# The fourth batch's softmax blocks turned by VectorE and moved by ScalarE, spread over two passes

## The chip, the cores and the metric

The kernel runs on one core of a Trainium2 chip. The metric is device time in microseconds (us) for one execution. The engines of the core are TensorE (PE, matrix products; its weight loads are listed apart as PEld), VectorE (DVE), ScalarE (ACT), GpSimd (POOL) and SyncE (SP, which here only issues transfers). Each works through its own queue in order, and they meet through semaphores.

## The reference

An attention with 32 learned memory slots per head, and on its output a mixture of 8 experts. Eight batches of 576 tokens, 8 heads of 64 features, so the model width is 512; experts have 1024 hidden units.

```python
def _attn_ref(q, k, v, phi):                      # phi: batch, head, token, 32 slots
    a = np.exp(phi - np.max(phi, axis=2, keepdims=True))     # softmax over the tokens
    a = a / (np.sum(a, axis=2, keepdims=True) + 1e-09)
    k_m = np.einsum('bhsm,bhsd->bhmd', a, k)      # 32 keys and values per head
    v_m = np.einsum('bhsm,bhsd->bhmd', a, v)
    scores = scale * np.matmul(q, k_m.transpose(0, 1, 3, 2))
    ...                                           # softmax over the 32 slots: attn
    return np.matmul(attn, v_m)

def _moe_ref(x, expert_emb, tau, w1, w2):
    ...                                           # cosine router: expert and gate of each token
    h = np.maximum(x[mask] @ w1[e], 0.0)
    out[mask] = gate_w[mask, None] * (h @ w2[e])
```

What matters here is the first softmax, over the tokens: its exponentials `exp(phi - max)` of one batch are 8 x 32 rows of 576 tokens, and the products with k and v contract over the tokens, so the exponentials are needed with the tokens on the partitions.

## The kernel before

The batches go through a software pipeline. Pass b (`batch(b, ...)`) runs the two layers of the chosen expert for batch b on TensorE and, between their steps, everything that later batches need. The first layer (`first`) has 16 steps of six matmuls (tiles ph, line 751); the second (`second`) has 40 steps: one half tile of 64 tokens x 2 and four full tiles of 128 tokens (py), eight steps each. In pass 0 the half tile comes first, in passes 1 to 6 behind the first full tile. `steps(b, t, u)` is an order written out by hand: a list of work for each place of `first` and `second`, which is emitted behind the matmuls of that step. An engine's queue therefore holds its instructions in exactly this order.

A tile py is emptied by ScalarE (ys, line 796), which multiplies by the gate. Four PSUM banks (`mm`) are used in rotation by ph, py and the four tiles pg of `project` (line 732), with which the next pass begins. `project` multiplies the first-layer weights by the slots' values; ScalarE casts each pg to gh (line 734), VectorE takes the rest gl (line 735), and both feed the first layer. Ahead of pg, at the start of pass 1, stand the transposes tk and tv; behind it the products ts and tl of the next batch's attention.

For batch m the exponentials are made in place in the buffer ex: `load_phi` brings phi, `largest` takes the maximum of a half (nm, line 481, VectorE), `softmax` the exponential with its sums (line 496, ScalarE). They are brought into the layout eT (tokens on partitions) in one of two ways:

- by TensorE (`blocks` and `flip`): 18 transposes into PSUM (line 533, tiles po and te) and four ScalarE copies (line 536);
- by VectorE and ScalarE (`blocks_of` and `by_token`): VectorE transposes 32 x 32 blocks of each half into xt (line 542), then ScalarE makes 16 moves, each a pair of copies that changes partitions (lines 550 and 552). The generator `self.moves` hands them out one at a time.

`slots` (line 574, from `gather`) then sums over the tokens. Before the change the first way serves the third batch (in pass 0) and the fourth batch (in pass 1, second-layer place 7); the second way serves the batches from the fifth on. The fourth batch's phi is issued by SyncE, at second-layer place 27 of pass 0; its maxima are taken at first-layer places 2 and 4 of pass 1 and its exponentials at second-layer places 0 and 1.

Other names that the steps touch: `norm` (line 181, VectorE, ea with sums s) and `root` and `gates` (ss, n, l; lines 248 to 279) compute the gates of the next batch's tokens. The power in `root` is GpSimd's, and l is an exponential on ScalarE. `parts` splits the attention weights (aT: a cast on VectorE, line 711, and a subtraction on GpSimd, line 712). At the end of pass 0 GpSimd sends out ys and then splits the next pass's second-layer weights (wh, wl).

Of the kernel before, what the change touches and what calls it, by code (L numbers as in the profile page):

```python
# [20 lines left out]
B, H, S, D, M = 8, 8, 576, 64, 32  # L21
N, DM, E, FF = B * S, H * D, 8, 1024
NG = 2
# [264 lines left out]
class Kernel:  # L288
# [136 lines left out]
    def load_phi(self, b, gs=range(NG)):  # L425
        if b < B:
            for g in gs:
                to = self.e(b, g)
                if g and 1 < b < 4:
                    self.nc.sync.dma_start(to[:, 64:], self.phiT[b, :, g, : 4 * P])  # L430
                    self.nc.sync.dma_start(to[:, :64], self.phiT[b, :, g, 4 * P :])
                else:
                    (self.nc.scalar if b == 4 else self.nc.sync).dma_start(to, self.phiT[b, :, g])

    def load_kv(self, b):
        if 1 < b < B:
# [363 lines left out]
    def steps(self, b, t, u):  # L800


        first, second = ([[] for _ in range(n)] for n in (16, 40))

        for j in range(8):
            at = first[j] if b else first[2] if j < 2 else first[3 + j] if j < 6 else first[8 + j]
            at.append(lambda j=j: self.split_w(self.nc.gpsimd.tensor_copy if b or j < 6 else None))
        if not b:
            late = t.late()
            first[0].append(lambda: t.norm(1))  # L810
            for g in range(NG):
                first[1].append(lambda g=g: self.part(g, slice(HS, S), self.nc.scalar.copy))
            first[1] += [lambda: t.norm(4), lambda: list(self.second_part)]
            first[2] += [lambda: t.turned(2, 3), t.total]
            first[3] += [lambda: t.norm(2, 3), lambda: self.load_kv(2)]
            for f in (4, 5, 6, 7):
                first[f].append(lambda: next(late))
            first[12] += [lambda: self.keep(0), lambda: self.load_q(2)]
        if u:
            c, o = b + 1, 0 if b else 3  # L820
            if not b:
                first[9].append(lambda: self.scores(c))
            for k in range(2):
                first[(3 + k if b else 9 + 2 * k)].append(lambda k=k: self.results(c, k))
            if not b:
                first[11].append(lambda: next(late))
                second[1].append(lambda: list(late))

            places = (first[6], first[8], first[10], first[12]), (first[12], first[14], second[0], second[2])
            if not b:  # L830
                places = (first[11], first[12], first[14], second[0]), (second[0], second[0], second[2], second[3])
            all = slice(0, BL)
            for g in range(NG):
                work = u.weigh((g,), all)
                places[g][0].append(lambda g=g: u.fill((g,), all, [self.sT[:, i] for i in range(NG)]))
                for at in places[g][1:]:
                    at.append(lambda work=work: next(work, None))
            for at, g in zip((second[0], second[2]) if b else (second[3], second[5]), range(NG)):
                at.append(lambda g=g: (u.divide((g,), all), u.lay(g), u.turn((g,), all)))
            m = b + 2  # L840
            if m < B:
                for g in range(NG):
                    if b < 2:
                        (first[2 + 2 * g] if b else second[2]).append(lambda g=g: self.largest(m, g))
                        second[g if b else 8 + g].append(lambda g=g: self.softmax(m, (g,)))
                second[4 if b else 9].append(lambda: self.shares(m))
                second[7 if b else 21].append(lambda: self.blocks(u, m, 1 if b else 0))
                second[15 if b else 21].append(u.pairs)
                if b:
                    second[15].append(lambda: self.sums_of(m, 1))  # L850
                if b > 1:
                    first[12].append(lambda: self.load_phi(m + 1))
                else:
                    second[7 if b else 27].append(lambda: self.load_phi(m + 1))
                second[15 if b else 24].append(lambda: self.gather(u, m))
                if b:
                    sides = self.by_feature(m)
                    second[16].append(lambda: next(sides))
                    for n in range(8):
                        second[17 + n] += [lambda: next(sides, None)] * 2  # L860
                if b > 1:
                    for at in ([first[9], first[11]] if b == 2 else []) + second[:8]:
                        at.append(lambda: next(self.moves, None))
                if b and m + 1 < B:
                    n0, n1, n2 = (16, 17, 20) if b == 1 else (8, 9, 16)
                    for g in range(NG):
                        second[n0].append(lambda g=g: self.largest(m + 1, g))
                        second[n1 + g].append(lambda g=g: self.softmax(m + 1, (g,)))
                        second[n2].append(lambda g=g: self.blocks_of(m + 1, g))
                    for n in (24, 25, 26, 27, 30, 31) if b == 1 else range(27, 35):  # L870
                        second[n].append(lambda: next(self.moves))
                second[22 if b else 35].append(lambda: self.load_kv(m + 1))
            else:
                second[15].append(u.attend)
                second[18].append(lambda: self.load_w2(u.choose(), 8))
                second[37].append(lambda: list(self.project(c, self.vT[c % 2], self.pt)))
            o = -4 if b else 0
            if not b:
                second[24] += [t.owner, t.flags]
            second[24 if not b else 20 if m == B else 18] += [u.owner, u.flags, self.parts]  # L880
            second[23 if b else 30].append(lambda: self.keep(c))
            for n, i in enumerate(((0, 1), (2, 3), (4,))):
                second[24 + n + o + (not b) + (m == B)].append(lambda i=i: u.norm(*i))
            after = u.late()
            for n in (27, 28, 29, 30, 31, 32):
                second[n + o].append(lambda: next(after))
            second[32 + o].append(lambda: list(after))
        return first, second
# [5 lines left out]
    def blocks(self, u, m, n):  # L894

        u.open()
        if m > 3:
            return
        ts = [self.free([P, 8, D], f"te{m}_{h}", h + n) for h in range(2)]
        self.flip(ts, [p[:, 3 * P : 3 * P + D] for p in u.ps[2:]])  # L900
# [294 lines left out]
```

## Time and profile before

| | us |
|---|---|
| median of 3 runs | 395.96 |
| lowest and highest run | 394.16, 396.05 |
| the profiled execution | 394.29 |
| its span, first to last instruction | 392.5 |
| PE busy | 383.3 (98%) |
| DVE busy | 243.3 (62%) |
| ACT busy | 203.2 (52%) |
| POOL busy | 186.5 (48%) |

The profile lists one execution. Pass 0's second layer lies at 46 to 77 us, pass 1 at 77 to 123 us. Busy shares are averages; for this change the timelines of single engines in these stretches are of more use, since they show the order in which an engine's queue runs, the idle time ahead of an instruction, and what ended it.

### The profile page before, as it was taken

How to read it: one execution, taken by the hardware profiler on the slowest of the kernel's cores; microseconds unless marked ns; L12 is line 12 of the kernel's file. 1: busy time of each engine (PE TensorE's matmuls, PEld its weight loads, DVE VectorE, ACT ScalarE, POOL GpSimd, SP SyncE). 2: the span in 40 equal slices, each digit the busy share in tenths (PEclk: the TensorE clock that was granted, in tenths of full speed). 3: DMA queues.
4: the chain of work that ended last, by engine and by line, in shares of the span. 5: the costliest groups of instructions: out<-in, count | busy, mean ns of one | idle time of the engine just before them, and what ended most of it. 6: DMA issues, size and time to landing. Idle time of an engine off the chain costs nothing. (4 is left out here: it accounts for less than half of the span.)

```text
span 392.5 us, 10269 instructions
## 1 busy us (share of the span) xinstructions
PE 383.3 (98%) x3837; PEld 310.1 (79%) x3837; DVE 243.3 (62%) x808; ACT 203.2 (52%) x622; POOL 186.5 (48%) x225
## 2 busy tenths in 40 slices
PE   8889999999999999999999999999999999999995
PEld 4458878799787977879787987879788897879883
DVE  5598994689573797348961798538952596535000
ACT  5376732176284785657656675667642751145011
POOL 0036940596153941569052951559242881529300
PEclk9999999999999999999999999999999999999998
DMA  7999936995789936997489915997379405890011
GB/s 269 395 352 358 379 86 159 337 384 233 164 235 381 403 85 148 344 378 277 89 251 368 405 68 111 330 392 282 66 173 365 149 3 109 282 363 0 30 53 43
DMA packets 68534, 91.24 MB, mean 232 GB/s; under 512 B 41112, under 2 KB 46744, under 8 KB 68352
## 3 DMA queue, kind: packets, MB, share of 16 engines
q1 hardware_dynamic: 65392, 81.61, 62.5%
q0 software_dynamic: 2688, 8.26, 5.9%
q10 hardware_dynamic: 400, 0.67, 0.7%
q8 instruction: 31, 0.51, 0.6%
q14 instruction: 23, 0.19, 0.1%
HBM read 71.19 MB, written 19.33 MB: 231 GB/s over the span
## 5 line engine op out<-in xcount | busy, mean ns | idle before, releaser
L751 PE MATMUL ph<-aT,gh 128*128 128x288 f32 x512 | 103.1, 296 | 0.0
L791 PE MATMUL py<-wh,hh 128*128 128x512 f32 x256 | 100.8, 394 | 0.0
L791 PE MATMUL py<-wl,hh 128*128 128x512 f32 x256 | 99.8, 390 | 0.0
L791 PE MATMUL py<-wh,hl 128*128 128x512 f32 x256 | 99.7, 389 | 0.0
L722 POOL TENSOR_TENSOR wl<-w2s,wh 128x512 fp32r<-128x512 f32 x64 | 83.3, 1302 | 5.1
L751 PEld LDWEIGHTS ph<-aT,gh 128*128 128x128 f32 x512 | 81.8, 188 | 1.8 <-DVE hl L758 0.8
L751 PE MATMUL ph<-aT,gl 128*128 128x288 f32 x256 | 75.4, 294 | 0.0
L755 ACT ACTIVATE hh<-ph 128x224 fp32r<-128x224 f32 (+1 forms) x128 | 48.8, 388 | 34.6 <-PE ph L751 34.1
L758 DVE SCALAR_TENSOR_TENSOR hl<-ph,hh 128x224 fp32r<-128x224 f32 (+1 forms) x128 | 51.8, 417 | 22.3 <-ACT hh L755 15.9
L796 ACT ACTIVATE ys<-py,gate 128x512 f32<-128x512 f32 (+1 forms) x40 | 25.8, 644 | 73.4 <-PE py L791 42.4
L963 POOL DMA_DIRECT2D out_dram<-ys x28 | 16.3, 582 | 92.4 <-ACT ys L796 87.2
L791 PEld LDWEIGHTS py<-wh,hh 128*128 128x128 f32 x256 | 48.1, 188 | 11.0 <-issue 1.4
L791 PEld LDWEIGHTS py<-wh,hl 128*128 128x128 f32 x256 | 48.1, 188 | 10.2
L791 PEld LDWEIGHTS py<-wl,hh 128*128 128x128 f32 x256 | 48.1, 188 | 9.4
L751 PEld LDWEIGHTS ph<-aT,gl 128*128 128x128 f32 x256 | 48.0, 188 | 0.0
L735 DVE TENSOR_TENSOR gl<-pg,gh 128x512 fp32r<-128x512 f32 x32 | 20.0, 684 | 42.2 <-ACT gh L734 42.2
L721 POOL CAST wh<-w2s 128x512 fp32r<-128x512 f32 x62 | 41.4, 668 | 0.1
L712 POOL TENSOR_TENSOR aT<-aw,aT 128x576 fp32r<-128x576 f32 (+1 forms) x18 | 23.5, 1319 | 32.0 <-DVE aT L711 27.9
L780 PE MATMUL py<-w2s,h 128*64 128x256 f32 x256 | 29.4, 382 | 0.0
L550 ACT COPY eT<-xt 32x256 f32<-32x256 f32 x64 | 25.8, 403 | 1.1
L780 PEld LDWEIGHTS py<-w2s,h 128*64 128x64 f32 x256 | 17.7, 137 | 10.4 <-DVE aw L100 1.8
L623 ACT COPY kv<-kt 32x64 f32<-32x64 f32 x80 | 19.4, 243 | 5.3 <-DVE kt L613 4.4
(173 smaller groups left out, 465.2 us busy)
## 6 DMA issues: line engine op xcount, KB each, us to landing
kx<-kv SPq DMA_DIRECT2D x32, 512.0 KB, 10.3
w2s<-w SPq DMA_DIRECT2D x28, 512.0 KB, 10.2
w1s<-w SPq DMA_DIRECT2D x28, 512.0 KB, 6.7
out_dram<-ys POOLq DMA_DIRECT2D x28, 256.0 KB, 6.4
qt<-qT SPq DMA_DIRECT2D x12, 576.0 KB, 9.7
ad<-aw SPq DMA_DIRECT2D x8, 576.0 KB, 11.1
td<-x SPq DMA_DIRECT2D x56, 72.0 KB, 2.4
ea<-td SPq DMA_DIRECT2D x7, 512.0 KB, 4.2
```

The costliest lines, as they stand in the source:

```text
L550: nc.scalar.copy(eT[to, :8, m].rearrange("p (g k) m -> p g k m", g=NG), xt[at, :, q : BL - 2 : 4])
L623: nc.scalar.copy(y, self.kt[32 * l : 32 * l + 32, g, h + 2 * i :: 2 - 4 * i])
L712: self.nc.gpsimd.tensor_tensor(out=al, in0=a, in1=ah.bitcast(F32), op=ALU.subtract)
L721: (copy or self.nc.scalar.copy)(h, x)
L722: self.nc.gpsimd.tensor_tensor(out=l, in0=x, in1=h.bitcast(F32), op=ALU.subtract)
L735: nc.vector.tensor_tensor(out=self.gl[:, g, f], in0=ps[g], in1=self.gh[:, g, f].bitcast(F32), op=ALU.subtract)
L751: nc.tensor.matmul(p, lhsT=w[:, g, fs], rhs=x[:, g, to], start=g == 0 and k == 0, stop=g == 1 and k == 2)
L755: nc.scalar.activation(self.hh[:, f, at], q, AF.Relu)
L758: nc.vector.scalar_tensor_tensor(out=self.hl[:, f, at], in0=q, scalar=0.0, in1=self.hh[:, f, at].bitcast(F32), op0=ALU.max, op1=ALU.subtract)
L780: nc.tensor.matmul(p[64 * j : 64 * j + 64], lhsT=self.h4[:, f], rhs=self.w2s[:, f, d * j : d * j + d], start=f == 0, stop=f == 7,)
L791: nc.tensor.matmul(p, lhsT=h[:, f, to], rhs=w[:, f], start=f == 0 and k == 0, stop=f == 7 and k == 2)
L796: nc.scalar.activation(y[:, :d], p, AF.Copy, scale=gate[:, i : i + 1])
```

## The change

The fourth batch goes over to the second way. Its phi is issued by ScalarE at place 22 of pass 0's second layer. Its maxima are taken at place 25, its exponentials at 26 and 27, and VectorE's block transposes stand at 28. Nine of the 16 moves stand at places 29 to 37 of pass 0's second layer; the other seven in pass 1, at first-layer places 9 and 11 and second-layer places 1, 3, 5, 7 and 9. The 18 transposes on TensorE and the four copies of pass 1 are gone.

```diff
-                if g and 1 < b < 4:
+                if g and b == 2:
...
-                    (self.nc.scalar if b == 4 else self.nc.sync).dma_start(to, self.phiT[b, :, g])
+                    (self.nc.scalar if b in (3, 4) else self.nc.sync).dma_start(to, self.phiT[b, :, g])
...
-                for g in range(NG):
-                    if b < 2:
-                        (first[2 + 2 * g] if b else second[2]).append(lambda g=g: self.largest(m, g))
-                        second[g if b else 8 + g].append(lambda g=g: self.softmax(m, (g,)))
+                if not b:
+                    for g in range(NG):
+                        second[2].append(lambda g=g: self.largest(m, g))
+                        second[8 + g].append(lambda g=g: self.softmax(m, (g,)))
...
-                    second[7 if b else 27].append(lambda: self.load_phi(m + 1))
+                    second[7 if b else 22].append(lambda: self.load_phi(m + 1))
...
-                if b > 1:
-                    for at in ([first[9], first[11]] if b == 2 else []) + second[:8]:
+                if b:
+                    for at in ([first[9], first[11]] if b < 3 else []) + (second[1:11:2] if b == 1 else second[:8]):
                         at.append(lambda: next(self.moves, None))
-                if b and m + 1 < B:
-                    n0, n1, n2 = (16, 17, 20) if b == 1 else (8, 9, 16)
+                if m + 1 < B:
+                    n0, n1, n2 = ((25, 26, 28), (16, 17, 20), (8, 9, 16))[min(b, 2)]
...
-                    for n in (24, 25, 26, 27, 30, 31) if b == 1 else range(27, 35):
+                    for n in (range(29, 38), (24, 25, 26, 27, 30, 31), range(27, 35))[min(b, 2)]:
                         second[n].append(lambda: next(self.moves))
...
-        if m > 3:
+        if m > 2:
             return
```

ScalarE at the end of pass 0, before: ys0_2 and ys0_3 are the outputs of the last two full tiles, l1 the gates' exponential, gh the cast of the first pg tile of pass 1.

```order
L796 ACTIVATE ys0_1_928<-py0_1_929,gate_98 128x512
L591 ACTIVATE ks_77<-acc2_1_1057,rs2_850 128x128
L796 ACTIVATE ys0_2_1032<-py0_2_1033,gate_98 128x512
L269 ACTIVATE l1_1158<-l1_1158 128x40
L796 ACTIVATE ys0_3_1172<-py0_3_1173,gate_98 128x512
L734 CAST gh_93<-pg1_00_1225 128x512
```

The same stretch of ScalarE now, from the exponentials of the fourth batch on (of the nine moves, pairs of L550 and L552, the first and the third are shown; one more stands ahead of ys0_2, six ahead of ys0_3).

```order
L496 ACTIVATE ex_69,sm3_1125<-ex_69,nm3_1124 128x576 x2
L550 COPY eT_76<-xt_85 32x8x32
L552 COPY eT_76<-xt_85 32x32
...
L796 ACTIVATE ys0_2_1034<-py0_2_1035,gate_98 128x512
L550 COPY eT_76<-xt_85 32x8x32
L552 COPY eT_76<-xt_85 32x32
L269 ACTIVATE l1_1170<-l1_1170 128x40
...
L796 ACTIVATE ys0_3_1186<-py0_3_1187,gate_98 128x512
L734 CAST gh_93<-pg1_00_1251 128x512
```

Two moves now stand ahead of ys0_2, all nine ahead of ys0_3 and of gh; the fourth pg tile waits for ys0_3, before and now.

VectorE in the same stretch, before: the casts aT, the norms (L181, the first and the last pair of ten), the sum ss and the reciprocal n behind GpSimd's root.

```order
L711 CAST aT_86<-aw 128x576 x2
L181 ISA ea,s_468<-po_0_948,ea 128x2x64
L181 ISA s_468 128x1
...
L181 ISA ea,s_468<-po_3_951,ea 128x2x64
L181 ISA s_468 128x1
L248 TENSOR_TENSOR ss_467<-s_468 128x5
L254 RECIPROCAL n_1141<-n_1141 128x5
```

VectorE now, in the same places.

```order
L711 CAST aT_86<-aw 128x576 x2
L481 TENSOR_REDUCE nm_1124<-ex 128x1 x2
L181 ISA ea,s_468<-po_0_948,ea 128x2x64
...
L181 ISA s_468 128x1
L248 TENSOR_TENSOR ss_467<-s_468 128x5
L542 STREAM_TRANSPOSE xt<-ex 128x576 x2
L254 RECIPROCAL n_1147<-n_1147 128x5
```

The two maxima stand ahead of the norms, and the block transposes behind ss; ScalarE's moves read what these transposes write.

TensorE in pass 1's second layer, before: from the last matmul of the first full tile (py1_0) over the transposes to the half tile (py1_4); of the 18 transposes the first four are shown.

```order
L791 MATMUL py1_0_1473<-wh_91,hl_96 128x512
L533 MATMUL po2_2_1537<-ident_133,ex_69 128x64
L533 MATMUL po2_3_1538<-ident_133,ex_69 128x64
L533 MATMUL te3_0_1539<-ident_133,ex_69 128x64
L533 MATMUL te3_1_1540<-ident_133,ex_69 128x64
...
L780 MATMUL py1_4_1566<-w2s_90,h4_97 64x256 x16
```

TensorE now, in the same place.

```order
L791 MATMUL py1_0_1498<-wh_91,hh_95 128x512
L791 MATMUL py1_0_1498<-wl_92,hh_95 128x512
L791 MATMUL py1_0_1498<-wh_91,hl_96 128x512
L780 MATMUL py1_4_1573<-w2s_90,h4_97 64x256 x16
L140 MATMUL po2_0_1564<-vv_82,aw_88 64x72
```

The half tile now follows the first full tile directly.

## Rows read from the trace of the kernel before

**Rows 1.** Page: PE's busy time, and the granted clock in 40 slices.
```profile
PE 383.3 (98%) x3837; PEld 310.1 (79%) x3837; DVE 243.3 (62%) x808; ACT 203.2 (52%) x622; POOL 186.5 (48%) x225
PEclk9999999999999999999999999999999999999998
```

**Rows 2.** Timeline, PE, start of pass 1 (start, duration, instruction, count).
```profile
77.35 1.95 PE L732 MATMUL pg<-w1s,kv 64*32 64x512 f32 x32
79.09 0.69 PE L652 MATMUL ts<-qt,kv 64*32 64x288 f32 x16
...
80.32 0.40 PE L751 MATMUL ph<-aT,gh 128*128 128x288 f32 x1
```

**Rows 3.** Timeline, ACT, same seam; in brackets idle time and releaser.
```profile
77.07 0.69 ACT L796 ACTIVATE ys<-py,gate 128x512 f32<-128x512 f32 x1 [2.18 <-PE py L791]
78.48 1.08 ACT L734 CAST gh<-pg 128x512 fp32r<-128x512 f32 x2 [0.72 <-PE pg L732]
```

**Rows 4.** Timeline, PE, pass 1, around the fourth batch's transposes.
```profile
98.40 0.39 PE L791 MATMUL py<-wh,hl 128*128 128x512 f32 x1
...
99.43 0.44 PE L780 MATMUL py<-w2s,h 128*64 128x256 f32 x2
```

**Rows 5.** Timeline, PE, pass 2, the same two tiles without transposes.
```profile
144.60 0.39 PE L791 MATMUL py<-wh,hl 128*128 128x512 f32 x1
144.92 0.44 PE L780 MATMUL py<-w2s,h 128*64 128x256 f32 x2
```

**Rows 6.** Timeline, DVE, end of pass 0: first norm, ss, n.
```profile
69.09 0.29 DVE L181 CUSTOM_DVE_ANT_1 ea<-po,ea 128x128 f32<-128x128 f32 x1
...
71.32 0.56 DVE L248 TENSOR_TENSOR ss<-s 128x5 f32<-128x5 f32 x1
73.88 0.19 DVE L254 RECIPROCAL n<-n 128x5 f32<-128x5 f32 x1 [2.00 <-POOL n L251]
```

**Rows 7.** Timelines, DVE, other places: two maxima, two block transposes, ss.
```profile
52.07 1.40 DVE L481 TENSOR_REDUCE nm<-ex 128x1 f32<-128x576 f32 x2
...
111.07 1.43 DVE L542 STREAM_TRANSPOSE xt<-ex 128x576 f32<-128x576 f32 x2
...
114.63 0.17 DVE L248 TENSOR_TENSOR ss<-s 128x5 f32<-128x5 f32 x1
```

**Rows 8.** Timeline, POOL, end of pass 0: the two subtractions.
```profile
68.96 2.90 POOL L712 TENSOR_TENSOR aT<-aw,aT 128x576 fp32r<-128x576 f32 x2 [3.82 <-DVE aT L711]
```

**Rows 9.** Timelines, ACT: an exponential; a first-layer step, moves, l, an output.
```profile
53.13 0.77 ACT L496 ACTIVATE ex<-ex,nm 128x576 f32<-128x576 f32 x1
...
88.55 0.36 ACT L755 ACTIVATE hh<-ph 128x224 fp32r<-128x224 f32 x1 [0.32 <-PE ph L751]
...
115.35 0.41 ACT L550 COPY eT<-xt 32x256 f32<-32x256 f32 x1
...
116.95 0.40 ACT L550 COPY eT<-xt 32x256 f32<-32x256 f32 x1
...
117.88 0.24 ACT L269 ACTIVATE l<-l 128x40 f32<-128x40 f32 x1 [0.40 <-DVE l L267]
...
118.69 0.69 ACT L796 ACTIVATE ys<-py,gate 128x512 f32<-128x512 f32 x1
```

**Rows 10.** ACT's copies in pass 0; landing of phi's loads; transfers by stretch.
```profile
60.62 1.07 ACT L536 COPY eT<-te 128x512 f32<-128x512 f32 x2 [0.17 <-PE te L533]
...
DMA to landing us min/median/max: 3.0/8.7/10.8
...
core 0: us, PE busy (x) PEld busy (x) DVE busy (x) ACT busy (x) POOL busy (x), PEclk, DMA share, GB/s
62.00:64.00 2.00, 2.00 (x9) 1.53 (x9) 0.89 (x5) 0.39 (x1) 0.00 (x0) 1.00 0.00 1
```

**Rows 11.** Busy time and clock by stretch (columns as in rows 10), the end.
```profile
388.00:390.00 2.00, 0.00 (x0) 0.00 (x0) 0.00 (x0) 0.39 (x1) 0.00 (x0) 1.00 0.18 42
390.00:392.00 2.00, 0.00 (x0) 0.00 (x0) 0.00 (x0) 0.00 (x0) 0.00 (x0) 0.62 0.13 32
```

## The prediction

> **What bounds the kernel now.** I read the page first, then the timelines of the stretches that the change touches. TensorE is busy for 383.3 of 392.5 us [rows 1], its granted clock is at its upper level in nearly every slice, and its queue runs strictly in the program's order, so the end moves by what the change takes off that queue and by every wait it puts into it. ScalarE and VectorE are half idle on average, but averages hide the place that matters here: the seam between pass 0 and pass 1. There TensorE goes from the last output tile of pass 0 to the four pg tiles (four PSUM banks, in rotation with the output tiles), then to ts and tl, then to the first layer [rows 2]. The third pg tile takes the bank of pass 0's third full output tile (ys0_2 empties it), the fourth that of the last one (ys0_3 empties it). Before, ScalarE does ys0_3 at 77.07 as soon as the tile is complete, and is idle ahead of it and ahead of the casts gh [rows 3]: the seam costs TensorE nothing, but the path is tight: the fourth pg tile starts at 77.35 + 3/4 x (79.09 - 77.35) = 78.66 [rows 2], 0.9 us after ys0_3 ends at 77.76.
>
> **What is removed from TensorE.** In pass 1's second layer the 18 turns of the fourth batch's exponentials go. From the start of the last matmul ahead of them to the start of the half tile's first is 99.43 - 98.40 = 1.03 us [rows 4]. In pass 2, where nothing stands between the same two, it is 144.92 - 144.60 = 0.32 us [rows 5]: a change of shape costs a bubble either way. So the gain is 0.71 us, not the 1 us that the group seems to take. It is a gain only if nothing else is late there: the half tile needs only operands that pass 1's first layer made long ago, and the moves of this batch are through (second-layer place 9) six places before the sums read them (place 15).
>
> **What is added to VectorE, and where it puts the first move.** In pass 0 two maxima come between the casts aT and the norms, which started at 69.09 [rows 6]. Two of them take 1.40 [rows 7]: the norms start at 70.49. They took 71.32 - 69.09 = 2.23 [rows 6], so ss starts at 72.72. Then ss, then the two transposes at 1.43 [rows 7], and only then can ScalarE move anything, since the first move reads both halves of xt.
> The small sum ss took 0.56 in this trace, and ended when GpSimd's two subtractions did, at 68.96 + 2.90 = 71.86 [rows 6, 8]; the same instruction in pass 1, with GpSimd not computing, took 0.17 [rows 7]. It now starts after 71.86, so I take 0.17: ss ends at 72.89, the transposes at 74.32. [...]
> The two exponentials (0.77 each, [rows 9]) run on ScalarE while VectorE does the 2.23 us of norms, so the transposes don't wait for them. The wait of VectorE for GpSimd's root is 2.00 long [rows 6]; the 1.43 of transposes lie in it, so the gates behind them are later only by the maxima and by ScalarE's exponential l.
>
> **What is added to ScalarE, and who waits for it.** The new order on ScalarE is: two moves, ys0_2, a move, l, six moves, ys0_3, then gh. A move is a pair of copies; from 115.35 to 116.95 there are three, 0.53 each; l takes 0.24, an output 0.69 [rows 9]. From 74.32: two moves 75.39, ys0_2 76.08, a move 76.61, l 76.85, six moves 80.05, ys0_3 80.74. Nothing of this waits for data: ys0_3's tile is complete when tk and tv begin, before 77.35 [rows 2], and the input of l is there 1 us later than before. TensorE's fourth pg tile waits for ys0_3, hence until 80.74 in place of 78.66: **a stall of 2.1 us**, and TensorE has no other work in its queue order. Behind the stall nothing is later still: gh starts at 80.74, and two casts take 1.08 [rows 3], while TensorE does the fourth pg tile, ts and tl for 0.44 + 1.23 us [rows 2]; so the first layer starts at about 82.4 with the first tile's gh and gl ready. VectorE's copies of tk, which ts needs, stand behind the gates, and these wait for l (76.85) and a handful of small operations; ts can't start before 81.2. GpSimd sends out ys0_3 and only then starts to split pass 1's second-layer weights; it is as late as TensorE is and keeps its lead.
> In pass 1 seven moves (3.7 us) replace four copies of turned blocks and two exponentials; ScalarE idles 0.32 us in a step of the first layer's second half [rows 9], a move overdraws that by 0.2, and four banks lie between ScalarE and TensorE there. I cost them at nothing. VectorE loses two maxima there, which costs or gains nothing at TensorE.
>
> **The transfer.** phi of the fourth batch is issued by ScalarE right behind the copies of pass 0's turned blocks, so at about 61 (the copies stand at 60.62, [rows 10]) in place of SyncE's queue, where it stood behind the weights. Its sequencer waits only for exponentials long done, so ys0_1 behind it isn't held. It must land by 69.09. Landings of such loads took 3.0 to 10.8 us, and the transfer engines were at 0.00 from 62 to 64 [rows 10]: I take it as landed by about 66. SyncE's queue loses the three issues; what stood behind them (stores and the next keys and values) comes earlier and is needed by nobody soon.
>
> **The sum.** -0.71 + 2.08 = **+1.4 us**. The profiled execution took 394.29 (span 392.5), so it would be 395.7 on its scale; it lies 1.67 below the median of the three runs, 395.96, and near the lowest, 394.16. Added to the median: **397.4**. The stall's own bounds: 1.6 if the nine moves run a tenth faster than in pass 1 (0.48), 2.9 if they run a tenth slower and ss still takes 0.56 in place of 0.17 (0.48 + 0.39). That is +0.9 to +2.2 for this case.
>
> **The rivals.**
> First, *the moves are hidden*: ScalarE reaches ys0_3 by 78.66 and only the gain is left, -0.7, 395.3 at the median (393.6 on the profile's scale). For it speaks that ScalarE idles in this stretch, 2.18 us ahead of ys0_3 alone [rows 3]. Against it: most of its idle time lies before 74.3, when the moves can't start; they would have to start 2.1 us sooner.
> Second, on the other side, *phi is late*: VectorE stops at the first maximum with the norms, ss and the gates queued behind it, ScalarE stops at the exponential, and every us past 69.09 adds one to the stall. With the longest landing of the trace, 61 + 10.8 = 71.8 for the second half, whose maximum was to start at 69.8, the stall is 2.0 longer: +3.4, 399.4. It decides from a landing of about 8 us; the empty transfer engines at 62 to 64 speak against it, the later transfers of pass 0 that share them (ea, w1s) for it.
> Third, *the clock falls*: TensorE is wholly idle for 2.1 us. At the trace's end it did nothing from 388 to 390 with the clock still at 1.00; from 390 to 392 the mean was 0.62 [rows 11], below full speed for a part of it. So the stall is about as long as an idle stretch that left the clock alone. [...]
> That the change doesn't do what it says I leave out: the instruction order shows the turns gone and the moves in place.
>
> **How the numbers follow.** Forecast 0.62, hidden 0.12, late phi 0.16, clock 0.06, anything else 0.04. About 0.5% (2.0 us) is what a measurement of this kernel can tell from no change. The forecast (+0.9 to +2.2) lies within it but for its upper end (0.07), hidden lies within it, late phi and clock mostly beyond: same 0.70, slower 0.27, faster 0.03. The range: from the hidden case at the median (395.3), a little lower for the spread of the runs, to the late-phi case: 395.0 to 399.3.
>
> **What would show it.** Right: TensorE idle for about 2 us ahead of the fourth pg tile, released by ys0_3; on ScalarE an unbroken row of moves from about 74.3 to 80; the half tile of pass 1 0.3 us behind its predecessor. Wrong: no idle time at pg (the moves run faster or start sooner), VectorE waiting for phi ahead of the maxima, a clock below 1.00 after the seam, or TensorE waits in pass 1's first layer that I have costed at nothing.

## The result and the profile after

The changed kernel is slower: 398.23 us median (397.5 to 399.54, 6 runs) against 394.6 for the kernel before in the same sessions (394.14 to 396.05, 6 runs), a ratio of 1.0079 with an interval of 1.0058 to 1.01, or +3.1 us (2.3 to 3.9). This ratio is the one on record with the runs; it is not the quotient of the two medians, which lie 3.6 us apart. The profiled execution took 398.35 with a span of 396.5 (before: 394.29 and 392.5). The forecast was +1.4 us. Its range, 395.0 to 399.3, held the time, but its own bounds for the change, +0.9 to +2.2, did not, and of the three classes the one that came, "slower by over 0.5%", had 0.27 against 0.70 for "same".

0.8 us of the 4.0 between the two profiles is no effect of the change. It arises before 31 us, in the start stage, where both programs are the same; TensorE waits there for the first loads (1.3 us in all for kx in the trace of after; 1.0 for kx and 1.2 for w1s in that of before), and from 12 to 16 us the mean granted clock was 0.67, where before's was 1.00; in the profiles of the eleven kernels told of here this stage was between 0.1 us shorter and 3.6 us longer than in the profile of before, without any order in the sizes. I therefore compare from 31 us on, and add 0.8 to a time of before to find it in the trace of after.

The page says little: TensorE has 18 matmuls fewer than in [rows 1] and is busy for longer; the ends of matmuls are modelled in these records, so their starts are what I go by.

```profile
PE 385.8 (97%) x3819; PEld 311.1 (78%) x3819; DVE 244.9 (62%) x810; ACT 210.4 (53%) x650; POOL 186.4 (47%) x225
```

The seam, TensorE's timeline of the kernel after (start, duration, instruction, count, in brackets idle time and releaser), answers [rows 2]:

```profile
78.19 1.92 PE L732 MATMUL pg<-w1s,kv 64*32 64x512 f32 x24
81.55 0.63 PE L732 MATMUL pg<-w1s,kv 64*32 64x512 f32 x4 [1.44 <-ACT ys L796]
81.58 0.69 PE L652 MATMUL ts<-qt,kv 64*32 64x288 f32 x8
82.00 0.61 PE L732 MATMUL pg<-w1s,kv 64*32 64x512 f32 x4
82.09 0.67 PE L652 MATMUL tl<-qt,kv 64*32 64x288 f32 x8
82.43 0.66 PE L652 MATMUL ts<-qt,kv 64*32 64x288 f32 x8
82.70 0.36 PE L660 MATMUL tl<-kv 64*32 64x72 f32 x8
82.91 0.66 PE L652 MATMUL tl<-qt,kv 64*32 64x288 f32 x8
83.40 0.30 PE L660 MATMUL tl<-kv 64*32 64x72 f32 x8
83.63 0.53 PE L751 MATMUL ph<-aT,gh 128*128 128x288 f32 x2
```

The fourth pg tile starts at 81.55. Undisturbed it would have started at 78.66 + 0.83 = 79.49 (the last matmul of the third tile starts at 79.52), so the stall is 2.06 us. What stands behind it no longer starts in the program's order: before, all 32 pg matmuls, then all ts, then all tl; now eights and fours of the three mixed. From the fourth pg tile to the first ph it takes 83.63 - 81.55 = 2.08, where before it took 80.32 - 78.66 = 1.66.

ScalarE's timeline over the same stretch, for [rows 3]:

```profile
74.99 0.40 ACT L550 COPY eT<-xt 32x256 f32<-32x256 f32 x1 [2.68 <-DVE xt L542]
...
80.26 0.40 ACT L550 COPY eT<-xt 32x256 f32<-32x256 f32 x1
80.57 0.21 ACT L552 COPY eT<-xt 32x32 f32<-32x32 f32 x1
80.81 0.69 ACT L796 ACTIVATE ys<-py,gate 128x512 f32<-128x512 f32 x1
81.39 2.04 ACT L734 CAST gh<-pg 128x512 fp32r<-128x512 f32 x4
```

From 74.99 on ScalarE has no idle time: nine moves, ys0_2 and l, and at 80.81 ys0_3, whose end lets the fourth pg tile go.

Pass 1, TensorE's timeline around the place of the removed turns, and the sums of the slots a little later, for [rows 4, 5]:

```profile
101.70 0.39 PE L791 MATMUL py<-wh,hl 128*128 128x512 f32 x1
102.01 3.67 PE L780 MATMUL py<-w2s,h 128*64 128x256 f32 x32
...
107.03 1.96 PE L574 MATMUL acc<-kx,eT 128*32 128x128 f32 x64
108.91 0.42 PE L574 MATMUL acc<-kl,eT 64*32 64x128 f32 x6
109.77 0.43 PE L574 MATMUL acc<-kl,eT 64*32 64x128 f32 x10 [0.44 <-issue]
```

The last sums of this run in the kernel before, and the same sums three passes later, before and after:

```profile
106.60 0.45 PE L574 MATMUL acc<-kl,eT 64*32 64x128 f32 x16
```
```profile
242.28 0.45 PE L574 MATMUL acc<-kl,eT 64*32 64x128 f32 x16
```
```profile
245.41 0.99 PE L574 MATMUL acc<-kl,eT 64*32 64x128 f32 x16
```

The half tile follows its predecessor by 0.31, as in pass 2 of the kernel before (0.32). But at 109.06 TensorE stops for 0.71 us, from start to start, in a run of short matmuls that wait for nothing the profile shows (the row's 0.44 counts from the modelled end). In the kernel before this run of 16 stands in one piece. The same happens at 245.57 (0.41 us).

Summed from 31 us: seam +2.47, turns -0.72, first hole +0.56 (0.71 less 0.15 that the kernel before loses a few matmuls earlier), second +0.54 (0.41, and 0.13 more in the order of the 16 around it), small steps elsewhere, most of them behind 246 us, +0.34 (0.19 of it at 371 us, where TensorE waits for weights that GpSimd splits); together +3.2, which agrees with the +3.1 of the timed runs.

### The profile page after: what moved, and what is told of

It is laid out like the page before. It is cut to its first block, busy times and chain, and to the rows that moved or that the text cites. A ratio compares the mean times of both kernels' runs of the same rounds, so it can differ in the third digit from the quotient of the medians.

```text
span 396.5 us, 10262 instructions
## 1 busy us (share of the span) xinstructions
PE 385.8 (97%) x3819; PEld 311.1 (78%) x3819; DVE 244.9 (62%) x810; ACT 210.4 (53%) x650; POOL 186.4 (47%) x225
## 5 line engine op out<-in xcount | busy, mean ns | idle before, releaser
L550 ACT COPY eT<-xt 32x256 f32<-32x256 f32 x80 | 32.3, 403 | 4.2 <-DVE xt L542 2.7
```

Of the source, the lines that this page charges most:

```text
L550: nc.scalar.copy(eT[to, :8, m].rearrange("p (g k) m -> p g k m", g=NG), xt[at, :, q : BL - 2 : 4])
```

## The experiments

Two questions were open: is the row of moves all that costs at the seam, and what are the holes? My first theory was that the moves hold ys0_3 (so their number decides) and that nothing else in the change costs. The rivals were that the early phi or the early exponentials cost by themselves, and that the removed turns win nothing.

**Five moves in pass 0 in place of nine** (the other eleven in pass 1):

```diff
-(second[1:11:2] if b == 1 else second[:8])
+(second[:8] + [second[9]] if b == 1 else second[:8])
-for n in (range(29, 38), (24, 25, ...
+for n in (range(29, 34), (24, 25, ...
```

> The changed kernel with five of the nine moves of pass 0 left there (places 29 to 33) and the other four put into pass 1 (second-layer places 0, 2, 4 and 6). Seam theory (the moves ahead of ys0_3 hold TensorE's fourth pg tile): four moves of 0.53 us fewer let ys0_3 end 2.1 us sooner, just when the tile could start, so the idle time at pg falls from 2.0 us to 0 to 0.2, the first layer of pass 1 starts 2.5 us sooner after pg than in the changed kernel, and with the 0.7 us of the removed turns it runs at 0.998 of the kernel before. Transfer theory (phi issued early, or the maxima and transposes in pass 0, cost the time): the ratio stays at 1.005 to 1.008.

**Twelve in pass 0** (three places with two):

```diff
-for n in (range(29, 38), (24, 25, ...
+for n in ([*range(29, 38), 35, 36, 37], (24, 25, ...
```

> The changed kernel with twelve moves in pass 0 (two each at places 35 to 37) and four in pass 1. Seam theory: three moves more, so the idle time at pg grows by 1.6 us to 3.6, and the time by 1.6 us over the changed kernel (+0.4%, ratio to before 1.012). If something else holds the seam (VectorE's gates or the copies of tk), the idle time stays at 2.0 us and the ratio at 1.008.

**The transfer alone**: the kernel before, with the fourth batch's phi issued by ScalarE at second-layer place 22. Its second half comes in the order that VectorE's way would want, so the turned blocks pair some tokens with other keys; the amount of work is the same.

```diff
-if g and 1 < b < 4:
+if g and b == 2:
-(self.nc.scalar if b == 4 else self.nc.sync)
+(self.nc.scalar if b in (3, 4) else self.nc.sync)
-second[7 if b else 27].append(lambda: self.load_phi(m + 1))
+second[7 if b else 22].append(lambda: self.load_phi(m + 1))
```

> The kernel before with one part of the change: phi of the fourth batch is issued by ScalarE at place 22 of pass 0's second layer; the turns stay on TensorE in pass 1. Seam theory: nothing but the transfers moves, ratio 1.000 within 0.003. Transfer theory: the earlier load and the shifted lanes of SyncE's queue cost 1 us or more, ratio 1.003 or above, with TensorE waiting for a load in pass 0 or 1.

**The turns' removal alone**: the kernel before, with the fourth batch's turns and their copies left out, so its sums use old blocks.

```diff
-        if m > 3:
+        if m > 2:
             return
         ts = [self.free([P, 8, D], f"te{m}_{h}", h + n) for h in range(2)]
```

> The kernel before without the fourth batch's 18 turns on TensorE and their four copies; that batch's slots are summed from stale blocks, the rest is as before. It prices the gain by itself. Seam theory: 0.71 us less, ratio 0.998, and the half tile of pass 1 starts 0.32 us after the last matmul of the tile ahead. Queue theory (the removed instructions shift TensorE's queue and open holes of 0.4 to 0.7 us in the short matmuls of the slots' sums, as the changed kernel shows at 109 and 245 us): holes in the sums show here too, and the ratio is 1.000 to 1.002.

The seam with five moves and with twelve, TensorE's timelines in this order:

```profile
78.10 2.29 PE L732 MATMUL pg<-w1s,kv 64*32 64x512 f32 x32
79.84 0.79 PE L652 MATMUL ts<-qt,kv 64*32 64x288 f32 x12
80.33 0.42 PE L652 MATMUL tl<-qt,kv 64*32 64x288 f32 x4
80.45 0.42 PE L652 MATMUL ts<-qt,kv 64*32 64x288 f32 x4
```
```profile
79.85 1.92 PE L732 MATMUL pg<-w1s,kv 64*32 64x512 f32 x24
84.80 0.63 PE L732 MATMUL pg<-w1s,kv 64*32 64x512 f32 x4 [3.03 <-ACT ys L796]
```

With five the stall is gone and 0.34 us are left, all of it in the mixed order of ts and tl; with twelve the seam costs 4.07, 1.60 more than with nine, and three moves are 3 x 0.53 = 1.6; from five to nine it is 2.13 for four moves, again 0.53 each. So the row of moves is the cause of the stall, move by move. With five the whole kernel was expected at 0.998 and came out at 1.0016, for the holes were not in that sum; the 1.012 expected with twelve lies in the interval around 1.0144. The early transfer changes nothing: from 31 us on that kernel's trace differs from before's by 0.0 us (ratio 0.9988, 0.9963 to 1.0013). The last one tells where the rest goes: the turns' time is won, yet the kernel has holes at 107.95 and 244.32 and comes out at 1.0022 (0.9997 to 1.0048), where 0.998 was expected if the removal won its 0.71 and opened no holes. The holes thus belong neither to phi nor to the moves: they come with the missing turns.

In all four kernels without the turns the first hole stands behind the record with index 2496 of TensorE's instructions (matmuls, weight loads and its sequencer's own, such as semaphore waits, counted from the start), the second behind 5312; the difference is 2816 = 11 x 256. And the trace has a queue for instructions, here on the page of the kernel after, and then among its transfers from 107.3 to 107.4 us (queue, packets, MB, share of the transfer engines):

```profile
q8 instruction: 31, 0.51, 0.5%
```
```profile
q8 instruction: 1, 0.02, 65.5%
```

31 reads of 16 KB, for 7714 records of TensorE: 249 a read. The second theory is therefore that **TensorE's queue is read in blocks, and TensorE runs dry when it finishes a block before the next has come**. 36 instructions fewer shift the program against the blocks, so that their ends fall into the runs of short matmuls. Blocks of 256 records agree with the 249 a read and with the distance of 11 x 256 between the holes; in these traces no hole stands at the ends of such blocks but at the few told of here, where 0.2 to 1.0 us show.

To test it I put 36 instructions back, far ahead, by writing three idle matmuls of 512 columns as 21 of 64 (in the last kernel of the four only 8, by seven of 192):

```diff
     k.load_phi(2)
-    k.warm(3)
+    k.warm(21, hot=k.mm([P, 64], "hot", 0))
```

The changed kernel with 36:

> The changed kernel, with the three idle matmuls of 512 columns ahead of the first batch written as 21 of 64 columns: 36 more instructions on TensorE's queue ahead of pass 0, as many as the removed turns took away, and 1344 columns for 1536. Theory (instruction blocks): in the changed kernel the trace has 16 KB reads of instructions at 107.32 and 243.43, and TensorE runs dry at 109.06 and 245.57 until 2.45 and 2.55 us after them; without the 36 instructions the blocks' ends fall inside the run of short matmuls of the slots. With the 36 back, both holes (0.71 and 0.42 us) are gone, the gap of the fourth pg tile stays at 2.0, and the kernel is 1.1 to 1.3 us shorter than the changed one: 1.004 to 1.006 of the kernel before. Rival (the holes come from the earlier phi or from transfers beside the sums): the holes stay where they are in the program, and the ratio is still 1.008.

Without turns, with 36:

> The kernel before without the fourth batch's turns and their copies (that part of the computation is left out), with the same 21 short idle matmuls for three long ones. Theory (instruction blocks): no hole at 108 or 244, and the 0.7 us that the turns took at half tile of pass 1 now shows in the whole: 0.9975 to 0.9995 of the kernel before, where it was 1.0022 without the pad. Rival (the holes have another cause): holes of 0.5 us as without the pad, 1.002.

Five moves, with 36:

> The changed kernel with five moves in pass 0 and eleven in pass 1, and the same 36 instructions on TensorE's queue. It had 1.0016 without them, 0.3 us left at the seam and 1.3 us of holes. Theory (instruction blocks and the seam are all the loss): -0.7 + 0.3 = -0.4 us, 0.9975 to 1.0 of the kernel before. Rival (something else in the change costs): 1.0015 or more.

The changed kernel with 8:

> The changed kernel with the three idle matmuls as seven of 192 columns: 8 more instructions on TensorE's queue. Theory (instruction blocks): both holes are still there but 8 instructions, four matmuls, earlier in the program: after four matmuls of the slots' last key sums where it was eight, and at the same instruction of the queue, counted from its start; sizes within 0.2 us of 0.71 and 0.42. Rival (the holes belong to a place of the program): after the eighth again.

The first hole in the changed kernel with 36 and with 8, TensorE's timelines:

```profile
106.56 1.72 PE L574 MATMUL acc<-kx,eT 128*32 128x128 f32 x52
108.61 0.63 PE L574 MATMUL acc<-kx,eT 128*32 128x128 f32 x12 [0.33 <-issue]
109.17 0.45 PE L574 MATMUL acc<-kl,eT 64*32 64x128 f32 x16
```
```profile
108.00 0.40 PE L574 MATMUL acc<-kl,eT 64*32 64x128 f32 x2
108.85 0.45 PE L574 MATMUL acc<-kl,eT 64*32 64x128 f32 x14 [0.45 <-issue]
```

With 8 the hole stands four matmuls earlier in the program (behind 2 listed kl matmuls, not 6), with 36 it stands among the kx matmuls, and in both it stands behind index 2496. It is tied to the count of instructions, not to a place of the program. The second hole is gone in all four; with 8 I had expected it to stay. And I had expected the first to go with 36 as well, and it went only with five moves: 0.60 and 0.35 us were left in the other two. The expected times were missed too: 1.009, 1.0006 and 1.0015, where 1.004 to 1.006, 0.9975 to 0.9995 and 0.9975 to 1.0 were expected; the last two have the expected values in their intervals, the first hasn't. The reads explain the holes that are left. From the trace's records, in us:

| kernel | read starts | index 2496 starts | TensorE goes on | read to going on |
|---|---|---|---|---|
| before | 103.63 | 105.89 | 106.04 | 2.41 |
| after | 107.32 | 109.06 | 109.77 | 2.45 |
| no turns | 106.22 | 107.95 | 108.51 | 2.29 |
| after, 36 | 106.18 | 108.01 | 108.61 | 2.43 |
| five moves, 36 | 106.89 | 109.10 | 109.28 | 2.39 |
| after, 8 | 106.59 | 108.13 | 108.85 | 2.27 |

In all twelve kernels TensorE goes on 2.26 to 2.49 us after the read of the block starts, and the hole is what is left of that when index 2496 is done. The kernel before stands at the edge: there the read starts 2.26 us ahead, and 0.15 us pass where a step is 0.1. At index 5312 the read starts 3.1 us ahead or more in every kernel with the count of before, and no hole is there; with 8 it starts 2.42 us ahead, which is just enough; with none 1.8 to 2.2 us ahead, and the holes are 0.2 to 0.6. What sets the start of a read within half a microsecond isn't settled: it comes while the run before is under way, and differs between kernels with the same count.

The other ends of blocks bear this out. One read belongs to each end (448, 704, and so on by 256, 29 of them up to 7616), and in all twelve traces it starts 5 us or more ahead of every end but three, and no hole stands there. The third of the three lies ahead of 31 us, so the sums here leave it out: behind index 704 = 2496 - 7 x 256, in the run of line 140, TensorE stands still for 0.2 to 0.8 us in every kernel but the one before the change, and goes on 2.26 to 2.57 us after the read starts. In the kernel before that read starts 3.4 us ahead, and there is no hole; with phi alone the program is the same up to there, and the hole is 0.44, so it too follows the start of the read. The changed kernel with 36:

```profile
29.05 0.96 PE L140 MATMUL po<-vv,aw 64*64 64x72 f32 x43 [0.61 <-issue]
```

The 36 instructions make this one longer: from 0.23 to 0.83 with nine moves, 0.52 to 0.66 with five, 0.68 to 0.82 with four, 0.24 to 0.83 without turns.

**Four moves in pass 0** (twelve in pass 1), with the 36 and without:

```diff
-(second[1:11:2] if b == 1 else second[:8])
+(second[:8] + second[9:11] if b == 1 else second[:8])
-for n in (range(29, 38), (24, 25, ...
+for n in (range(29, 33), (24, 25, ...
```

> The changed kernel with four moves in pass 0 and twelve in pass 1, and the 21 short idle matmuls for three long ones. Theory (the row of moves ahead of the second half's scores and the instruction blocks are all that the change costs): with a move of 0.53 us less than with five, the fourth pg tile waits for nothing, the scores' two row halves run in step as before, and the 0.34 us that five moves left at the seam is gone; no hole at index 2496 or 5312; what remains is the 0.7 us of the turns: 0.997 to 0.9995 of the kernel before. Rival (the earlier exponentials and phi cost something on their own): 1.001 or more.

> The same without the short idle matmuls: four moves in pass 0, twelve in pass 1. Theory (row of moves and instruction blocks): nothing is lost at the seam, the turns' 0.7 us are won in pass 1, and the two holes at index 2496 and 5312 of TensorE's queue (0.5 to 0.85 and 0.3 to 0.6 us) and 0.2 at the end take it back: 1.000 to 1.003 of the kernel before. Rival (no holes, if they hang on the seam's delay): 0.998.

The seam of the one with 36, TensorE's and ScalarE's timelines:

```profile
78.32 1.95 PE L732 MATMUL pg<-w1s,kv 64*32 64x512 f32 x32
80.06 0.69 PE L652 MATMUL ts<-qt,kv 64*32 64x288 f32 x16
80.55 0.69 PE L652 MATMUL tl<-qt,kv 64*32 64x288 f32 x16
```
```profile
78.28 0.69 ACT L796 ACTIVATE ys<-py,gate 128x512 f32<-128x512 f32 x1
79.45 2.05 ACT L734 CAST gh<-pg 128x512 fp32r<-128x512 f32 x4 [0.49 <-PE pg L732]
```

ScalarE now waits for pg and not the other way round, the sixteens stand in one piece again, and the seam costs 0.0 in both traces. But with the 36 a hole of 0.52 was left at 2496, where none was expected; without them it was 1.01 us, the largest of all, where 0.5 to 0.85 was expected. All kernels, by stretch of the trace against the kernel before (us), and by the timed runs:

| kernel | seam | turns | at 2496 | at 5312 | rest | sum from 31 us | ratio (95%) |
|---|---|---|---|---|---|---|---|
| after | 2.47 | -0.72 | 0.56 | 0.54 | 0.34 | 3.2 | 1.0079 (1.0058 to 1.01) |
| five moves | 0.34 | -0.72 | 0.70 | 0.41 | 0.26 | 1.0 | 1.0016 (0.9988 to 1.0044) |
| twelve moves | 4.07 | -0.72 | 0.62 | 0.71 | 0.02 | 4.7 | 1.0144 (1.0097 to 1.0192) |
| phi alone | 0 | 0 | 0 | 0 | 0 | 0.0 | 0.9988 (0.9963 to 1.0013) |
| no turns | 0 | -0.59 | 0.42 | 0.61 | 0.16 | 0.6 | 1.0022 (0.9997 to 1.0048) |
| after, 36 | 2.47 | -0.74 | 0.45 | 0 | 0 | 2.2 | 1.009 (1.0063 to 1.0116) |
| no turns, 36 | 0 | -0.71 | 0.21 | 0 | 0 | -0.5 | 1.0006 (0.9976 to 1.0036) |
| five moves, 36 | 0.34 | -0.72 | 0.03 | 0 | 0 | -0.3 | 1.0015 (0.9989 to 1.0041) |
| after, 8 | 2.47 | -0.74 | 0.58 | 0 | 0 | 2.3 | one run |
| four moves, 36 | 0 | -0.71 | 0.38 | 0 | 0 | -0.3 | 0.9993 (0.9966 to 1.0021) |
| four moves | 0 | -0.71 | 0.86 | 0.32 | 0.4 | 0.9 | 1.0007 (0.998 to 1.0034) |

In the row without turns, -0.59 is -0.71 at the half tile and a step of +0.11 at 89.6 us, whose cause is open.

The timed runs bear out the seam: the interval of nine moves lies above those of four and five, and that of twelve above it but for a touch (1.0097 against 1.01). They don't resolve the holes. The 36 instructions win 1.0 to 1.3 us from 31 us on in four pairs of traces, of which the longer hole at 704 takes back 0.1 to 0.6. The ratios of those pairs differ by +0.0011 (nine moves), -0.0001 (five), -0.0014 (four) and -0.0016 (no turns), with an interval of about 0.0026 to either side on each ratio; in the first pair the time even points the other way. So the holes are shown in the traces, one execution each, and their size in the median is open. No version here is measurably faster than the kernel before; four moves with 36 instructions has the lowest ratio of those with the change in it, and can't be told from it.

## Why the prediction was right or wrong

**The gain in pass 1 (-0.71)**: right where it was read, -0.72. "It is a gain only if nothing else is late there" was the right condition with the wrong list: I looked for operands and banks, and it was TensorE's own instructions that came late, with holes of 0.71 and 0.41 us.

**VectorE and the first move (74.32)**: right. With the 0.83 of the start stage it would be 75.15; it was 74.99. The maxima took 1.40 at 69.90, the transposes 1.43 at 73.52, and ss took 0.17, not 0.56: it started at 73.44, and GpSimd's subtractions had ended at 69.77 + 2.91 = 72.68.

```profile
69.90 1.40 DVE L481 TENSOR_REDUCE nm<-ex 128x1 f32<-128x576 f32 x2
...
73.44 0.17 DVE L248 TENSOR_TENSOR ss<-s 128x5 f32<-128x5 f32 x1
73.52 1.43 DVE L542 STREAM_TRANSPOSE xt<-ex 128x576 f32<-128x576 f32 x2
```

**ScalarE's row and the stall (2.08)**: right: 80.81 for ys0_3 where the working gives 80.05 + 0.83 = 80.88, and a stall of 2.06.

**"Behind the stall nothing is later still"**: wrong, and the first mis-sized term: 2.08 should have been 2.47. It rested on a queue that "runs strictly in the program's order", and behind the wait the starts do not keep that order: the first ts stand at 81.58, the last four pg, which the program has ahead of them, at 82.00. I took 0.44 + 1.23 for the fourth pg tile, ts and tl from [rows 2], where they run in one piece; behind the wait they ran in mixed order and took 2.08. The loss goes with the mixed order and not with the wait's length: with five moves TensorE isn't idle there, the order is mixed, and 0.34 is lost; with four the order is whole and nothing is lost. What mixes the order when hardly anything waits was not tried.

**"In pass 1 seven moves cost nothing"**: right. Eleven and twelve cost nothing either: no step between 84 us and the half tile but the turns' own.

**The transfer**: right. phi landed at most 3.9 us after its issue at 61.55 and 62.01, so by 65.9, and the rival of a late phi falls; the transfer alone costs 0.0.

```profile
DMA to landing us min/median/max: 3.6/3.7/3.9
```

**The clock**: that rival falls too. The seam by stretches in the kernel after, and the stall of the kernel with twelve moves (busy time of PE, PEld, DVE, ACT, POOL, then the granted clock, DMA share and GB/s):

```profile
80.00:82.00 2.00, 0.56 (x16) 0.31 (x20) 0.00 (x0) 1.96 (x7) 0.21 (x1) 1.00 1.05 409
82.00:84.00 2.00, 2.00 (x59) 1.30 (x39) 2.00 (x4) 1.43 (x3) 1.91 (x3) 1.00 1.11 373
```
```profile
82.00:84.00 2.00, 0.00 (x0) 0.00 (x0) 0.00 (x0) 1.97 (x8) 0.00 (x0) 1.00 1.02 412
86.00:90.00 4.00, 4.00 (x56) 3.63 (x48) 2.66 (x5) 1.92 (x5) 3.83 (x5) 1.00 1.04 361
```

From the last start of a matmul to the next, TensorE stood for 2.03 us in the first and 3.62 us in the second (1.44 and 3.03 by the modelled ends). The granted clock stays at 1.00 in all these rows. No run shows what a fall of the clock would cost at the seam; that it would lie "mostly beyond" the 0.5% was my assumption. The lower clock of the start stage, 0.67 from 12 to 16 us in the kernel after with TensorE at work, lies ahead of the 31 us from which I compare.

**The sum**: +1.4 became +3.1. Missing were, by the trace, 0.39 behind the stall and 1.4 of holes and small steps: TensorE's own instructions stood in the sum at nothing. No rival stood for the holes. That the time lies only 0.8 above the forecast of 397.4, and inside the range, is in part luck. The forecast was added to 395.96, the median of three runs, and the six runs of the same sessions put the kernel before at 394.6; and the range reached up to 399.3 for a late phi, which did not come. As a change the forecast was 1.7 us too low. Nothing in the views I had read of before pointed to the holes, though the page did list a queue of 31 instruction reads, and the gap of 0.15 at index 2496 was there to be seen.

## What to carry to other kernels

Work that is moved to a half-idle engine is priced by the next thing that engine must empty: count back from the time at which the bank is wanted, here 78.66, and see how many moves fit: 78.66 less 74.32, two outputs and l leaves 2.7 us, room for five; five lost 0.34 in the runs and four nothing, where nine were put. Behind a stall, don't price the following matmuls as if they ran undisturbed: those of 64*32 in the rows took 2.08 us here from the fourth pg tile to the first ph, where it was 1.66. And when instructions go from a queue that feeds long runs of short matmuls, look at where its blocks now end: part of a gain can go back there, far from the edit, as here 0.71 and 0.41 us at 109 and 246 us.

## What the runs showed of the hardware that was not expected

The traces list 31 reads of instructions of 16 KB, one for 249 of TensorE's 7714 records in the kernel after, and at the holes TensorE goes on 2.26 to 2.57 us after such a read starts; in the runs of short matmuls it had got to the indices below 1.4 to 2.3 us after that start. The holes were 0.2 to 1.0 us, the longer ones named "issue" in the timeline, and always behind the same three indices of the queue, 704, 2496 and 5312, multiples of 256 apart. At the seam the matmuls of 64*32 in the rows, once their order was mixed, took 0.34 to 0.42 us longer for the same work.
